# Where TensorE's side visits stand in a step, and a small matrix inverse in array tiles of 32 by 32

## The chip, the core and the metric

The kernel runs on one core of one Trainium2 chip. The metric is the device time of one execution in microseconds, as the median of several runs. A profiled execution shows each engine's instructions: TensorE (PE, and PEld for its weight loads), VectorE (DVE), ScalarE (ACT), GpSimd (POOL) and SyncE (SP), which issues most of the transfers.

## What is computed

Landmark (Nystrom) attention for 8 batches of 8 heads, then a dense two-layer network, then a mixture of 8 experts where each token goes to one expert.

```python
# attention, per batch and head: S = 576, D = 64, m = 32 landmarks
q_lm, k_lm = means of q and k over segments of 18
A, Bm, C = softmax(q k_lm^T), softmax(q_lm k_lm^T), softmax(q_lm k^T)
Z = Bm^T / (norm1(Bm) * norminf(Bm) + 1e-6)
for _ in range(6):
    Z = 2 * Z - Z @ Bm @ Z
x = A @ Z @ C @ v
# dense: (4608, 512) x (512, 2048), leaky relu 0.01, x (2048, 512)
# experts: argmax of x @ w_gate; out = gate * (relu(xe @ w1[e]) @ w2[e]), F = 1024
```

## The kernel before

TensorE's main work is a row of *steps*. A dense step ("m", 16 for each of 8 batches) does one 128-wide slice of the hidden layer: the first layer of the step two ahead (`h_mm`, L545, two halves of 288 columns, each of six matmuls) and then the second layer of this step (`o_mm`, L595, four *blocks* of 128 tokens, each of three matmuls: high by high, low by high, high by low). In batch 0 the second layer is plain fp32 (L590, one matmul per block). After each odd batch four short steps ("x", L604) finish the 64 tokens left over from two batches; then come the expert steps ("e", 8 per slot, with L899 for the first layer and L595, L921 for the second).

Everything else that TensorE does is a *visit*. The attention of batch b is cut into parts, and `PLAN` gives each a position in steps, counted from the start of batch b-1; `gate_plan` does the same for the gate's parts, and the tables at L1110 to L1122 for the experts' gathers. `side` turns the fraction of a position into a turn: an "m" step has 8, after each half of a half of the first layer (turns 0 to 3) and after each block (turns 4 to 7). An "e" step has 9, an "x" step 4. The engines execute in the order in which this loop writes, so a part that waits holds up whatever is written behind it on its engine.

The parts that matter here, for a batch b:

- `qk_load`, `red`: loads of q and k, and VectorE's sums over segments (L272), into `kT` and `qlm`
- `sc` 1 and `sc` 0: scores of landmarks against the keys' second and first half (L279, by `eight`), which need all of the reductions; `b_*` and `c_*`: softmax of them
- `et`, `tv`: transposes of C's scores (L365, L368) and C v (L378, 4 column tiles of 32)
- `n_g`, `n_k` 0 to 5, `n_y`, `n_w`: the inverse. Four heads lie on the partitions in groups of 32. To multiply four 32 by 32 matrices in one 128 by 128 matmul, VectorE spreads them into a block-diagonal matrix `rbd` with a mask `m4b` (L410, L437, L451, L458)
- `sa`, `a_*`: A's scores and softmax, transposed and split into `at`
- `u_mm`: the combined matrix times `w_in`, into `ub`, which the first layer of batch b reads; each takes two `wi` tiles, and loads the next two (`wi_load`)
- `xt_tr`, `logits`, `logits_t`, `g_l2`, `g_l3`, `g_l4`, `g_sc`: the gate of the batch before. `s_xt`: transposes of gathered expert tokens (L867)

Visits share two PSUM banks, `psw0` and `psw1` (from the experts on, one); the first layer has two, `hps`, and the blocks four. Batch 0's attention runs ahead of the steps, in the order of `FIRST`. Between its parts, and in the steps of batch 0, *ticks* convert the 64-bit weights: ScalarE L191 and L195, VectorE L199 and L203, GpSimd L216.

Of the kernel before, what the change touches and what calls it, by code (L numbers as in the profile page):

```python
# [66 lines left out]
def kernel(  # L67
# [100 lines left out]
    XE = 0.2  # L168
    XS = .4
# [231 lines left out]
    def b_nrm(b):  # L401
        bl, nn = A.pop((b, "bl")), A.pop((b, "nn"))
        bb = A[b, "bb"] = small("bb", [128, 2, 2, LM])
        DVE.tensor_reduce(out=nn[:, 2:4], in_=bl, axis=AX.X, op=ALU.add)
        DVE.tensor_scalar(out=nn[:, 2:4], in0=nn[:, 2:4], scalar1=1e-9, scalar2=None, op0=ALU.add)
        DVE.reciprocal(out=nn[:, 2:4], in_=nn[:, 2:4])
        DVE.tensor_tensor(out=bb[:, 0], in0=bl, in1=bcm(nn[:, 2:4]), op=ALU.mult)
        DVE.transpose(out=bb[:, 1].rearrange("p g m -> p (g m)"), in_=bb[:, 0].rearrange("p g m -> p (g m)"))
        rb = A[b, "rb"] = small("rbd", [128, 2, 4, LM], 2)
        DVE.tensor_tensor(out=rb, in0=bc4(bb[:, 1]), in1=m4b, op=ALU.mult)  # L410

    def n_g(b):
# [18 lines left out]
        DVE.tensor_tensor(out=gs, in0=ps[:, :2 * LM].rearrange("p (g m) -> p g m", g=2),  # L431
                          in1=bcm(cc), op=ALU.mult)
# [65 lines left out]

    PLAN = [
# [5 lines left out]
        (4.6, c_exp, 0), (4.75, c_exp, 1), (4.9, b_nrm), (5.2, c_rec, 0), (5.25, et, 0, 0), (5.26, et, 0, 1),
        (5.76, tv, 0), (5.77, et, 1, 0), (5.8, v_load, 1), (6.0, c_rec, 1), (6.26, et, 1, 1), (6.27, n_g),
        (6.76, sa, 0), (7.38, sa, 1), (7.7, a_max, 0), (7.75, a_sub, 0), (8.01, tv, 1), (8.02, n_k, 0),
        (8.25, a_exp, 0), (8.3, a_max, 1), (8.4, a_sub, 1), (8.63, n_k, 1), (8.8, a_sum, 0), (8.9, a_exp, 1),
        (9.0, a_mul, 0), (9.26, n_k, 2), (9.4, a_sum, 1), (9.5, a_mul, 1), (9.88, n_k, 3), (10.05, a_tr, 0),
        (10.2, a_hi, 0), (10.3, a_lo, 0), (10.51, n_k, 4), (10.7, a_tr, 1), (10.85, a_hi, 1), (10.95, a_lo, 1),  # L510
        (11.13, n_k, 5), (11.15, wi_load, 0), (11.3, wi_load, 1), (11.63, n_y), (12.13, n_w), (12.63, u_mm, 0),
        (13.88, u_mm, 2), (15.13, u_mm, 4), (18.13, u_mm, 6),
# [597 lines left out]
    for s in range(NSLOT):  # L1110
        t0 = T1 + NF * s
        x = t0 - 1 - XE - 5 * XS
        if s == 0:
            p = t_early + 0.4
        else:
            p = max(t_rest + 0.5 if s == KA else 0, x - 2.5)
        if s == 1:
            p = max(p, T1 - 2)
            x = max(x, p + 1)
        put([(p, part(s_tab, s))])  # L1120
        put([(p + 0.6 if j < XGB else x + XS * (j - XGB) + 0.1, part(s_gather, s, j)) for j in range(5)])
        put([(x + XS * j, part(s_xt, s, j)) for j in range(5)])  # L1122
# [169 lines left out]
```

## Time and profile before

| | us |
|---|---|
| median of 3 runs (1291.85 to 1292.27) | 1292.18 |
| the profiled execution | 1291.29 |
| its span | 1289.5 |
| TensorE busy in the span | 1227.5 (95%) |
| VectorE busy | 609.0 (47%) |
| ScalarE busy | 512.9 (40%) |
| GpSimd busy | 468.8 (36%) |

The span is what the profile's rows cover; 1.8 us of the execution lie around it. Matmuls overlap, each starting before the one before has left the array, so a step is best read from one start to the next. Of TensorE's busy time 383.8 us are L595 with `gh` and 253.4 us are L545. Times in the rows count from the start of the span.

### The profile page before, as it was taken

The page shows a single profiled execution, that of the slowest core. Times are in us where ns is not written, and L with a number is a line of the kernel's source. Part 1 is how long each engine was busy: PE and PEld are TensorE (multiplying, and loading weights), DVE is VectorE, ACT ScalarE, POOL GpSimd, SP SyncE. Part 2 cuts the span into 40 slices and gives each one's busy share as a digit, 9 for nine tenths or more (in the row PEclk, how much of TensorE's full clock was granted, in tenths as well). Part 3 has the DMA queues.
Part 4 walks back from the last instruction along what each step waited for, and adds up shares of the span by engine and source line. Part 5 has one row for each costly group of instructions (what it writes and reads, how often), then busy time and mean ns, then how long its engine had stood idle before and what let it go on. Part 6 is the DMA issues. An engine that isn't in the chain of part 4 may idle for free.

```text
span 1289.5 us, 22321 instructions
## 1 busy us (share of the span) xinstructions
PE 1227.5 (95%) x8630; PEld 1006.5 (78%) x8630; DVE 609.0 (47%) x1546; ACT 512.9 (40%) x1117; POOL 468.8 (36%) x362
## 2 busy tenths in 40 slices
PE   5788999999999999999999999999999999999994
PEld 2545567877877887878887888789989999999993
DVE  7788566535455435465435443244353332333311
ACT  3455355444344343344343444542343343333211
POOL 1544324433423424423424334624353333333201
PEclk9989999999999999999999999999999999999997
DMA  7677462351151241151141122341454334433001
GB/s 254 232 246 238 147 233 60 115 166 53 34 190 52 66 166 52 36 188 52 67 165 52 41 92 90 120 139 34 156 175 157 122 103 140 131 120 109 21 31 39
DMA packets 61891, 151.04 MB, mean 117 GB/s; under 512 B 10192, under 2 KB 19664, under 8 KB 61776
## 3 DMA queue, kind: packets, MB, share of 16 engines
q1 hardware_dynamic: 54736, 130.61, 30.8%
q0 software_dynamic: 7040, 18.92, 4.5%
q8 instruction: 70, 1.15, 0.4%
q14 instruction: 45, 0.37, 0.1%
HBM read 121.87 MB, written 27.63 MB: 116 GB/s over the span
## 4 chain that ended last, share of the span: by engine, by line
PE 79%; DVE 9%; issue 4%; ACT 1%; DMA 0%; POOL 0%; POOLq 0%; SPq 0%; DVEq 0%; ACTq 0%
PE acc L595 34%; PE hps L899 14%; PE hps L545 14%; PE psw L279 3%; PE acc L604 3%; PE psw L921 2%; PE acc L590 2%; PE psw L445 1%; PE psw L867 1%; PE psw L634 1%; DVE kT L272 1%; DVE qlm L272 1%; PE psw L378 1%; DVE te L199 1%; PE psw L642 1%
## 5 line engine op out<-in xcount | busy, mean ns | idle before, releaser
L595 PE MATMUL acc<-wo,gh 128*128 128x512 f32 x1216 | 383.8, 397 | 0.0
L562 POOL TENSOR_TENSOR gl<-hs,gh 128x512 fp32r<-128x512 f32 x112 | 147.1, 1313 | 311.5 <-ACT gh L561 183.2
L595 PEld LDWEIGHTS acc<-wo,gh 128*128 128x128 f32 x1216 | 217.6, 188 | 48.2 <-issue 11.7
L545 PE MATMUL hps<-at,ub 128*128 128x288 f32 x1536 | 253.4, 307 | 1.6 <-DVE hs L551 1.5
L545 PEld LDWEIGHTS hps<-at,ub 128*128 128x128 f32 x1536 | 220.9, 191 | 33.7 <-issue 20.0
L595 PE MATMUL acc<-wo,gl 128*128 128x512 f32 x608 | 238.0, 391 | 0.0
L551 DVE TENSOR_TENSOR hs<-hps,hs 128x288 f32<-128x288 f32 x224 | 98.9, 451 | 130.0 <-ACT hs L549 129.8
L908 DVE SCALAR_TENSOR_TENSOR gl<-hps,gh 128x288 fp32r<-128x288 f32 (+1 forms) x128 | 54.0, 423 | 197.3 <-ACT gh L904 197.3
L595 PEld LDWEIGHTS acc<-wo,gl 128*128 128x128 f32 x608 | 114.2, 188 | 25.0
L549 ACT ACTIVATE hs<-hps 128x288 f32<-128x288 f32 x256 | 101.9, 414 | 74.3 <-PE hps L545 71.1
L904 ACT ACTIVATE gh<-hps 128x288 fp32r<-128x288 f32 x128 | 52.8, 412 | 176.1 <-PE hps L899 111.6
L561 ACT CAST gh<-hs 128x512 fp32r<-128x512 f32 x112 | 69.5, 620 | 119.0 <-PE acc L595 94.4
L855 POOL DMA_INDIRECT xg<-x_d,gi x40 | 41.6, 1041 | 132.4 <-DVE gi L847 61.1
L940 POOL DMA_INDIRECT out_dram<-rows,gi x40 | 40.6, 1015 | 124.8 <-DVE rows L938 75.8
L492 DVE TENSOR_TENSOR ub<-psw,ub 128x512 fp32r<-128x512 f32 (+1 forms) x70 | 41.3, 632 | 70.0 <-ACT ub L491 70.0
L899 PE MATMUL hps<-xt,wo 128*128 128x288 f32 x480 | 68.7, 297 | 0.0
L899 PE MATMUL hps<-at,wo 128*128 128x288 f32 x480 | 68.0, 296 | 0.0
L899 PEld LDWEIGHTS hps<-xt,wo 128*128 128x128 f32 x480 | 66.4, 188 | 1.6
L899 PEld LDWEIGHTS hps<-at,wo 128*128 128x128 f32 x480 | 65.8, 188 | 1.6
L491 ACT CAST ub<-psw 128x512 fp32r<-128x512 f32 (+1 forms) x70 | 34.6, 547 | 65.6 <-PE psw L279 65.6
L595 PE MATMUL acc<-ub,gh 128*128 128x512 f32 x192 | 59.8, 393 | 0.0
L887 POOL TENSOR_TENSOR wo<-wraw,wo 128x1024 fp32r<-128x1024 f32 x20 | 48.0, 2398 | 23.3 <-ACT wo L883 23.0
(244 smaller groups left out, 1805.0 us busy)
## 6 DMA issues: line engine op xcount, KB each, us to landing
wraw<-in_moe_w_dram SPq DMA_DIRECT2D x64, 512.0 KB, 4.1
wi<-wi_d SPq DMA_DIRECT2D x56, 512.0 KB, 4.5
kT<-in_k_dram SPq DMA_DIRECT2D x32, 288.0 KB, 5.1
qT<-in_q_dram SPq DMA_DIRECT2D x32, 288.0 KB, 5.3
raw<-in_moe_w_in_dram SPq DMA_DIRECT2D x16, 512.0 KB, 5.2
vraw<-in_v_dram SPq DMA_DIRECT2D x16, 512.0 KB, 5.4
raw<-in_moe_w_out_dram SPq DMA_DIRECT2D x16, 512.0 KB, 4.6
x_d<-rows SPq DMA_DIRECT2D x32, 256.0 KB, 3.3
```

The source lines that it names most:

```text
L492: DVE.tensor_sub(out=u[:, :, 1, :], in0=p3, in1=u[:, :, 0, :].bitcast(F32))
L545: PE.matmul(out=ps[:, :HT], lhsT=us[:, wl, c:c + 128], rhs=at[:, al, 2 * (b % 2) + g, c0:c1], start=(n == 0), stop=(n == 5))
L549: ACT.mul(out=hs[:, c0:c1], in_=ps[:, :HT], mul=0.01)
L551: DVE.tensor_max(out=dst[:, c0:m], in0=ps[:, :m - c0], in1=hs[:, c0:m])
L561: ACT.copy(out=gh[:, :512], in_=src)
L562: POOL.tensor_tensor(out=gl, in0=src, in1=gh[:, :512].bitcast(F32), op=ALU.subtract)
L595: PE.matmul(out=acc(key, j), lhsT=g[hl][:, j * 128:(j + 1) * 128], rhs=wsel[:, wl, :], start=(f == 0 and i == 0), stop=(f == nf - 1 and i ...
L855: POOL.indirect_dma_start(out=xg[:n, :], out_offset=None, in_=x2_d[0:rows, :], in_offset=IND(ap=M[s, "gi"][:n, 0, j:j + 1], axis=0), bound ...
L887: (POOL if n % 2 else DVE).tensor_tensor(out=r[:, :, 1], in0=raw.rearrange("p (f c) -> p f c", f=2), in1=r[:, :, 0].bitcast(F32), op=ALU.s ...
L899: PE.matmul(out=ps[:, :HT], lhsT=wr[:, wl, d * 128:(d + 1) * 128], rhs=xt[:, al, d, c0:c1], start=(n == 0), stop=(n == 11))
L904: ACT.activation(out=gh[:, c0:c1], in_=ps[:, :HT], func=AF.Relu)
L908: DVE.scalar_tensor_tensor(out=lo, in0=ps[:, a - c0:b - c0], scalar=0.0, in1=gh[:, a:b].bitcast(F32), op0=ALU.max, op1=ALU.subtract)
```

## The change

Two things change. First, positions: in `PLAN`, `gate_plan` and the experts' table, visits of TensorE get positions that end in .51 or .88 (turn 4, behind the first block, and turn 7, behind the last), where they had any turn. Their other parts move along. Second, the inverse is no longer done with block-diagonal matrices. `diag` multiplies the four heads' 32 by 32 matrices as four matmuls, each on its own rows and columns of the array (partitions 32p to 32p+32), which write one PSUM bank at different partitions. The addition of the former Z is a further matmul with the identity `C["eye"]`, accumulated in PSUM, and one ScalarE copy takes the result out; VectorE's masked copies, copies and additions in `n_k` are gone, and the masks in `b_nrm` and `n_g`. `FIRST` is the same.

```diff
+    def diag(out, lhs, rhs, start=True, stop=True):
+
+        for p in range(4):
+            h = slice(32 * p, 32 * p + 32)
+            PE.matmul(out=out[h], lhsT=lhs[h], rhs=rhs[h], start=start, stop=stop, skip_group_check=True)
...
     def n_k(b, i):
-        rx, rb = A[b, "rx"], A[b, "rb"]
+
+        rx = A[b, "rx"]
         lo, hi = {0: (0, 1), 5: (1, 2)}.get(i, (0, 2))
         ps = psw()
         for g in range(2):
-            PE.matmul(out=ps[:, 64 * g + LM * lo:64 * g + LM * hi], lhsT=rb[:, g].rearrange("p h m -> p (h m)"),
-                      rhs=rx[:, g, lo:hi, :])
-        p4 = ps[:, :128].rearrange("p (g a m) -> p g a m", g=2, a=2)
-        nx = small("rx", [128, 2, 2, LM], 2)
-        nb = small("rbd", [128, 2, 4, LM], 2)
-        if i < 5:
-            DVE.tensor_tensor(out=nb, in0=bc4(p4[:, :, 0, :]), in1=m4b, op=ALU.mult)
-            DVE.tensor_copy(out=nx[:, :, 0, :], in_=p4[:, :, 0, :])
-        if i > 0:
-            DVE.tensor_tensor(out=nx[:, :, 1, :], in0=p4[:, :, 1, :], in1=rx[:, :, 1, :], op=ALU.add)
-        else:
-            DVE.tensor_copy(out=nx[:, :, 1, :], in_=rx[:, :, 1, :])
-        if i == 5:
-            DVE.tensor_tensor(out=nb, in0=bc4(nx[:, :, 1, :]), in1=m4b, op=ALU.mult)
-        A[b, "rx"], A[b, "rb"] = nx, nb
+            c, m, e = 64 * g + LM * lo, 64 * g + LM, 64 * g + 2 * LM
+            diag(ps[:, c:c + LM * (hi - lo)], rx[:, g, 0, :], rx[:, g, lo:hi, :], stop=hi == 1)
+            diag(ps[:, m:e], C["eye"], rx[:, g, 1, :], start=hi == 1)
+        nx = A[b, "rx"] = small("rx", [128, 2, 2, LM], 2)
+        ACT.copy(out=nx[:, :, lo:, :], in_=ps[:, :128].rearrange("p (g a m) -> p g a m", g=2, a=2)[:, :, lo:, :])
...
-        (3.625, sc, 1), (4.125, sc, 0), (4.0, b_max), (4.3, c_max, 0), (4.5, c_max, 1), (4.52, b_exp),
+        (3.88, sc, 1), (4.2, b_max), (4.4, b_exp), (4.88, sc, 0), (5.05, c_max, 0), (5.15, c_exp, 0), (5.2, c_max, 1),
...
-        P += [(t, g_l2), (t + 0.1, g_l3), (2.88 + NX * (b % 2), g_l4), (3.4 + NX * (b % 2), g_sc)]
+        P += [(t, g_l2), (t + 0.1, g_l3), (3.51 + NX * (b % 2), g_l4), (4.0 + NX * (b % 2), g_sc)]
...
-        x = t0 - 1 - XE - 5 * XS
+        xp = [t0 + x for x in (-3.45, -3.08, -2.45, -2.08, -1.45)]
```

Three places show how the order moves, all in batch 5, which carries batch 6's attention.

TensorE at `sc` half 1, before. `acc0` to `acc3` are the step's blocks, `hps` its first layer, `psw` the visit's banks; the visit's eight matmuls (two banks, four heads' `kT`) stand as their first and last:

```order
L545 MATMUL hps_6344<-at_84,ub_83 128x288 x6
L595 MATMUL acc0_6144<-wo1_1560,gh_6252 128x512 x2
L595 MATMUL acc0_6144<-wo1_1560,gl_6253 128x512
L595 MATMUL acc1_6150<-wo1_1560,gh_6252 128x512 x2
L595 MATMUL acc1_6150<-wo1_1560,gl_6253 128x512
L279 MATMUL psw0_6372<-kT_6109,qlm_6218 32x320
...
L279 MATMUL psw1_6373<-kT_6172,qlm_6218 32x320
L595 MATMUL acc2_6156<-wo1_1560,gh_6252 128x512 x2
```

The same place of TensorE after, with `g_l4`'s two matmuls (L679, L680) in the same step:

```order
L580 MATMUL acc0_6581<-wo1_1710,gl_6688 128x512
L679 LDWEIGHTS ltri_b_87
L679 MATMUL psw1_6792<-oh_6705,ltri_b_87 128x32
L680 LDWEIGHTS ones_b_88
L680 MATMUL psw1_6792<-ohc_6706,ones_b_88 128x32
...
L580 MATMUL acc3_6612<-wo1_1710,gl_6688 128x512
L276 MATMUL psw0_6816<-kT_6559,qlm_6661 32x320
...
L276 MATMUL psw1_6817<-kT_6610,qlm_6661 32x320
L530 MATMUL hps_6839<-at_84,ub_83 128x288 x6
```

The visit moved from behind the second block to behind the fourth, and `g_l4` into its step, behind the first block.

VectorE ahead of that visit, before: the last two reductions (L272) stand behind `g_l4`'s eight instructions (L702 to L710), the first and last of which are shown:

```order
L272 TENSOR_REDUCE qlm_6218<-qT_6154 128x32
L702 TENSOR_REDUCE pay_6319<-gex_6237 128x4
...
L706 TENSOR_TENSOR grk_6316<-psw1_6313,cst_81 128x32
...
L710 CAST gpi_6318<-gpf_6317 128x4
L272 TENSOR_REDUCE kT_6172<-kT_6172 128x32
L551 TENSOR_TENSOR hs_6333<-hps_6334,hs_6333 128x288
L272 TENSOR_REDUCE qlm_6218<-qT_6178 128x32
```

VectorE at the same place after:

```order
L269 TENSOR_REDUCE kT_6610<-kT_6610 128x32
L536 TENSOR_TENSOR hs_6768<-hps_6769,hs_6768 128x288
L269 TENSOR_REDUCE qlm_6661<-qT_6628 128x32
L536 TENSOR_TENSOR hs_6768<-hps_6779,hs_6768 128x288
L687 TENSOR_REDUCE pay_6798<-gex_6704 128x4
...
L691 TENSOR_TENSOR grk_6795<-psw1_6792,cst_81 128x32
```

The reductions moved ahead of the gate's chain.

TensorE between the first and the second `u_mm` of that batch, before (from the last matmul of the one to the first of the other):

```order
L279 MATMUL psw0_6952<-wi_6892,wt_86 32x256
L595 MATMUL acc2_6156<-wo6_2325,gh_6864 128x512 x2
L595 MATMUL acc2_6156<-wo6_2325,gl_6865 128x512
L595 MATMUL acc3_6174<-wo6_2325,gh_6864 128x512 x2
L595 MATMUL acc3_6174<-wo6_2325,gl_6865 128x512
L545 MATMUL hps_6989<-at_84,ub_83 128x288 x6
L545 MATMUL hps_6998<-at_84,ub_83 128x288 x6
L595 MATMUL acc0_6144<-wo6_2325,gh_6917 128x512 x2
...
L595 MATMUL acc3_6174<-wo6_2325,gl_6918 128x512
L279 MATMUL psw1_7019<-wi_6973,wt_86 32x256
```

The same stretch of TensorE after:

```order
L276 MATMUL psw0_7483<-wi_7390,wt_86 32x256
L530 MATMUL hps_7514<-at_84,ub_83 128x288 x6
L530 MATMUL hps_7523<-at_84,ub_83 128x288 x6
L580 MATMUL acc0_6581<-wo6_2434,gh_7442 128x512 x2
...
L580 MATMUL acc3_6612<-wo6_2434,gl_7443 128x512
L276 MATMUL psw1_7544<-wi_7504,wt_86 32x256
```

Six blocks between the two visits became four. In the same way the inverse's steps, one visit each, moved to turns 4 and 7; there two matmuls became sixteen, of 64 and of 32 columns. In the trace each fp32 matmul is two records.

## Rows read from the trace of the kernel before

**Rows 1.** Stretches: length, busy us (instructions) of each engine, clock, transfers.

```profile
14.00:46.50 32.50, 18.55 (x191) 13.16 (x191) 28.25 (x73) 13.96 (x30) 12.47 (x10) 1.00 0.58 196
46.50:141.00 94.50, 83.82 (x531) 49.55 (x524) 76.40 (x177) 50.07 (x110) 44.73 (x34) 0.95 0.71 235
141.00:820.00 679.00, 671.53 (x5189) 539.38 (x5190) 341.13 (x934) 290.64 (x710) 247.24 (x199) 1.00 0.30 101
```

**Rows 2.** TensorE in order of time (start, us, what), batch 6's `sc` visits.

```profile
577.93 0.76 PE L279 MATMUL psw<-kT,qlm 64*32 64x320 f32 x12
...
580.58 0.73 PE L595 MATMUL acc<-wo,gh 128*128 128x512 f32 x2
...
582.96 0.72 PE L279 MATMUL psw<-kT,qlm 64*32 64x288 f32 x16
583.60 0.66 PE L545 MATMUL hps<-at,ub 128*128 128x288 f32 x3
```

**Rows 3.** TensorE in order of time, the first and last of the six visits.

```profile
191.93 1.16 PE L279 MATMUL psw<-kT,qlm 64*32 64x320 f32 x12
...
195.33 0.73 PE L595 MATMUL acc<-wo,gh 128*128 128x512 f32 x2
...
680.58 0.76 PE L279 MATMUL psw<-kT,qlm 64*32 64x320 f32 x12
...
682.58 0.74 PE L595 MATMUL acc<-wo,gh 128*128 128x512 f32 x2
```

**Rows 4.** VectorE in order of time, ahead of that visit.

```profile
575.86 0.18 DVE L702 TENSOR_REDUCE pay<-gex 128x4 f32<-128x32 f32 x1
...
578.09 0.75 DVE L272 TENSOR_REDUCE kT<-kT 128x32 f32<-128x576 f32 x1
```

**Rows 5.** VectorE in order of time, one step of batch 0's inverse.

```profile
29.50 0.42 DVE L451 TENSOR_TENSOR rbd<-acc,cst 128x256 f32<-128x256 f32 x1
29.84 0.21 DVE L452 COPY rx<-acc 128x64 f32<-128x64 f32 x1
...
30.10 0.74 DVE L300 TENSOR_REDUCE amx<-st 128x18 f32<-128x576 f32 x1
```

**Rows 6.** A stretch behind a long wait of TensorE, as in rows 1.

```profile
91.00:97.00 6.00, 6.00 (x52) 3.00 (x51) 2.06 (x7) 2.55 (x6) 2.59 (x2) 0.67 0.13 49
```

**Rows 7.** TensorE in order of time, first and second `u_mm` of batch 6.

```profile
629.63 1.09 PE L279 MATMUL psw<-wi,wt 64*32 64x256 f32 x32
...
632.15 1.76 PE L545 MATMUL hps<-at,ub 128*128 128x288 f32 x12
633.75 0.62 PE L595 MATMUL acc<-wo,gh 128*128 128x512 f32 x2
...
636.26 0.39 PE L595 MATMUL acc<-wo,gl 128*128 128x512 f32 x1
636.58 1.09 PE L279 MATMUL psw<-wi,wt 64*32 64x256 f32 x32
637.61 1.86 PE L545 MATMUL hps<-at,ub 128*128 128x288 f32 x12
639.30 0.63 PE L595 MATMUL acc<-wo,gh 128*128 128x512 f32 x2
```

**Rows 8.** SP's issue of two `wi` tiles; landing of all from 200 to 800.

```profile
637.35 0.80 SPq L238 DMA_DIRECT2D wi<-wi_d  x2
...
DMA to landing us min/median/max: 3.5/4.5/5.9
```

**Rows 9.** TensorE in order of time, around one step of batch 6's inverse.

```profile
608.67 0.39 PE L595 MATMUL acc<-wo,gl 128*128 128x512 f32 x1
...
609.81 0.39 PE L595 MATMUL acc<-wo,gl 128*128 128x512 f32 x1
```

**Rows 10.** A stretch within one `tv` visit, as in rows 1.

```profile
591.52:591.97 0.45, 0.45 (x33) 0.44 (x32) 0.00 (x0) 0.00 (x0) 0.00 (x0) 1.00 0.00 0
```

**Rows 11.** TensorE in order of time, in batch 7's remainder steps.

```profile
831.13 0.66 PE L634 MATMUL psw<-cst,rows 128*128 128x128 f32 x4 [2.04 <-DVE xt L870]
```

More of the change, by code (lines that the diff above doesn't have):

```diff
@@ L160, in wo @@
         return wo_t[f // 2][:, f % 2]
-    XE = 0.2
-    XS = .4
     XGB = 3
@@ L408, in b_nrm @@
         DVE.transpose(out=bb[:, 1].rearrange("p g m -> p (g m)"), in_=bb[:, 0].rearrange("p g m -> p (g m)"))
-        rb = A[b, "rb"] = small("rbd", [128, 2, 4, LM], 2)
-        DVE.tensor_tensor(out=rb, in0=bc4(bb[:, 1]), in1=m4b, op=ALU.mult)
     def n_g(b):
-        bb, rb = A[b, "bb"], A.pop((b, "rb"))
-        ps = A[b, "gps"] = psw()
+        bb = A[b, "bb"]
+        ps = psw()
         for g in range(2):
-            PE.matmul(out=ps[:, g * LM:(g + 1) * LM], lhsT=rb[:, g].rearrange("p h m -> p (h m)"),
-                      rhs=bb[:, 1, g, :])
+            diag(ps[:, 64 * g:64 * g + LM], bb[:, 1, g, :], bb[:, 1, g, :])
         nn = small("nn2", [128, 2, 2])
         DVE.tensor_reduce(out=nn, in_=bb, axis=AX.X, op=ALU.add)
-        nbt = small("rbd", [128, 2, 4, LM], 2)
+        nbt = small("nbt", [128, 2, 4, LM])
         nb, nt = nbt[:, 0], nbt[:, 1]
@@ L430, in n_g @@
         gs = small("bl", [128, 2, LM])
-        DVE.tensor_tensor(out=gs, in0=ps[:, :2 * LM].rearrange("p (g m) -> p g m", g=2),
+        DVE.tensor_tensor(out=gs, in0=ps[:, :128].rearrange("p (g m) -> p g m", g=2)[:, :, :LM],
                           in1=bcm(cc), op=ALU.mult)
@@ L503 @@
         (2.4, red, 'k', 2), (2.65, red, 'q', 2), (3.0, red, 'k', 3), (3.25, red, 'q', 3),
-        (3.625, sc, 1), (4.125, sc, 0), (4.0, b_max), (4.3, c_max, 0), (4.5, c_max, 1), (4.52, b_exp),
[L505 to L512, printed above, removed]
+        (3.88, sc, 1), (4.2, b_max), (4.4, b_exp), (4.88, sc, 0), (5.05, c_max, 0), (5.15, c_exp, 0), (5.2, c_max, 1),
+        (5.3, b_nrm), (5.4, c_exp, 1), (5.6, c_rec, 0), (5.88, et, 0, 0), (5.89, et, 0, 1),
+        (6.51, tv, 0), (6.52, et, 1, 0), (6.55, v_load, 1), (6.7, c_rec, 1), (6.88, et, 1, 1), (6.89, n_g),
+        (7.51, sa, 0), (8.51, sa, 1), (8.7, a_max, 0), (8.75, a_sub, 0), (8.88, tv, 1), (8.89, n_k, 0),
+        (9.1, a_exp, 0), (9.15, a_max, 1), (9.25, a_sub, 1), (9.51, n_k, 1), (9.6, a_sum, 0), (9.7, a_exp, 1),
+        (9.8, a_mul, 0), (9.88, n_k, 2), (10.1, a_sum, 1), (10.2, a_mul, 1), (10.51, n_k, 3), (10.6, a_tr, 0),
+        (10.88, n_k, 4), (10.9, a_hi, 0), (11.0, a_lo, 0), (11.15, wi_load, 0), (11.2, a_tr, 1), (11.3, wi_load, 1),
+        (11.51, n_k, 5), (11.6, a_hi, 1), (11.7, a_lo, 1), (11.88, n_y), (12.51, n_w), (12.88, u_mm, 0),
+        (13.88, u_mm, 2), (14.88, u_mm, 4), (18.51, u_mm, 6),
     ]
@@ L1115 @@
         else:
-            p = max(t_rest + 0.5 if s == KA else 0, x - 2.5)
+            p = max(t_rest + 0.5 if s == KA else 0, xp[0] - 2.5)
         if s == 1:
             p = max(p, T1 - 2)
-            x = max(x, p + 1)
+            xp = [max(x, p + 1 + i / 100) for i, x in enumerate(xp)]
         put([(p, part(s_tab, s))])
-        put([(p + 0.6 if j < XGB else x + XS * (j - XGB) + 0.1, part(s_gather, s, j)) for j in range(5)])
-        put([(x + XS * j, part(s_xt, s, j)) for j in range(5)])
+        put([(p + 0.6 if j < XGB else xp[j - XGB] + 0.1, part(s_gather, s, j)) for j in range(5)])
+        put([(xp[j], part(s_xt, s, j)) for j in range(5)])
     def first_u0(_, s):
```

25 lines of the change are left out of this document (9 added, 16 removed).

## Prediction

> **What bounds the kernel now.** I read the table of stretches first. From 141 to 820 us TensorE is busy 671.53 of 679.00 us, so there only what TensorE executes and waits for counts. Before that it is not the bound: VectorE is busy 28.25 of 32.50 us from 14 to 46.5 us (87%, TensorE 57%), and 76.40 of 94.50 us from there to 141 us (81%) [rows 1]. The first stretch is the inverse of batch 0 with the conversion of the weights; the second is plain batch 0, with batch 1's attention and the rest of the conversion beside it. So the change is costed by two rules: VectorE's instructions before 141 us, TensorE's spacing after it.
>
> In the TensorE-bound part I read visits from start to start, because matmuls overlap and "idle" shows only part of a stall. One visit per batch waits for long: `sc` with half 1. In the fifth of the six steady batches (2 to 7) it holds the blocks back from 577.93 to 580.58 us, 2.65 us, where the other half, which waits for nothing, takes 582.96 to 583.60, 0.64 us [rows 2]. The first takes 3.40 us and the last 2.00 us [rows 3]; the four between are 2.00, 2.64, 2.00 and 2.65. VectorE's last `qlm` ends the wait, and it is late because the gate's `g_l4` chain, from 575.86 to 578.09 us, 2.23 us, stands in VectorE's queue ahead of the last two reductions [rows 4]. Together the six waits cost 14.69 - 6 x 0.64 = 10.85 us; half 1 is 32 columns wider, which takes off some 0.3: **10.5 us**.
>
> **The change part by part.**
>
> *Removed VectorE work.* A full step of the iteration occupies VectorE from 29.50 to 30.10 us, 0.60 us: the masked copy 0.34, the copy and the addition 0.13 each [rows 5]. Per attention the change takes away four such steps (2.40), step 0 (mask, two copies: 0.60), step 5 (addition and mask: 0.47) and two more masks (0.68), 4.15 us in all; ScalarE gets six small copies, and has room. For batch 0 all this lies in the stretch where VectorE is busy 87% of the time, so I take 0.87 x 4.15 = 3.6 us: **-3.6** (bounds 0, if the chain through ScalarE and TensorE takes over, and -4.2). For batch 1, 0.81 x 4.15 = 3.4 us, less some of TensorE's added work (below): **-3.0**. Its bounds are wide, since all visits of batch 1 also move, most of them later: +2 if VectorE then waits for TensorE's results, -7 if the long stalls go too; after one of them TensorE runs 6 us at a granted 0.67 of its clock, between its levels of 1.2 and 2.4 GHz, where 1.00 would need 4 us [rows 6]. From batch 2 on VectorE's saving is worth nothing, as TensorE sets the pace.
>
> *`sc` moved.* Half 1 goes from behind a step's second block to behind its fourth, 2 x 0.68 = 1.37 us later, and `g_l4` goes behind the last reduction, which takes 2.23 us out of its way. Together 3.6 us, more than the longest wait of 2.76. What is late next is the PSUM bank: `g_l4` now holds one of the two `psw` banks three blocks before `sc` wants both, and VectorE reads it some 1.8 us into its chain. I leave 0.3 us for that: **-10.2** (bounds -10.5 and -6, if the bank costs most of a microsecond each time).
>
> *`u_mm` moved.* The second and third of these visits come one step after the one before. Now 629.63 to 636.58, 6.95 us, holds a step and two blocks more. A step without a visit takes 636.58 - 632.15 = 4.43 us, the visit itself 637.61 - 636.58 = 1.03 [rows 7], so the new spacing is 5.5 us. Their `wi` tiles are asked for 0.77 us after the visit starts (637.35 against 636.58), the second 0.45 later, and land 4.5 us after issue, 5.9 at most [rows 8]: the second is there 5.7 to 7.1 us after the visit's start, and is wanted at 5.5 + 0.5 = 6.0. SP's queue is not otherwise held. That is 0 to 1.1 us of waiting, twice in each of six batches; the median says nothing, the maximum 1.1, and I take 0.3: **+3.5** (0 to +13).
>
> *The inverse in array tiles.* A step's visit now costs TensorE 609.81 - 608.67 = 1.14, less three matmuls at 0.228: 0.46 us [rows 9]. It was 4 matmul records; steps 0 to 5 become 32 records, `n_g` and `n_y` 16, each on one of four diagonal tiles. No row shows 32 by 32 tiles. The nearest is `tv`, four column tiles side by side: 32 weight loads and matmuls of 64 columns in 0.45 us, so a round of four takes 56 ns [rows 10]. The fixed price of a visit in tiles I take from `u_mm`: 636.26 to 639.30 is 3.04, less a plain first layer (633.75 - 632.15 = 1.60) and one matmul (0.23): 1.21 us; its four rounds of 256 columns take 0.89 at `tv`'s rate, which leaves 0.32 [rows 7]. So steps 1 to 4 cost 0.32 + 4 x 0.056 + 4 rounds of 32 columns at 0.028 to 0.056, 0.66 to 0.77: +0.20 to +0.31 each. Step 5 is +0.08 to +0.31, `n_y` about 0, step 0 (behind `tv`) and `n_g` (behind `et`) -0.05 to +0.25 each. Sum per batch +0.75 to +2.1; I take 1.2, nearer the low end because `tv`'s rounds go with its columns. Times six: **+7.2** (+4.5 to +12.6).
>
> *Expert steps.* `s_xt` moves from between first-layer quarters to behind blocks. Only stalls can change: one of 2.04 us in batch 7's remainder steps [rows 11], where three transposing visits still share two banks. **-0.5** (-2.3 to +1.5).
>
> Sum: -3.6 - 3.0 - 10.2 + 3.5 + 7.2 - 0.5 = -6.6 us. The profiled execution took 1291.29 us, 0.89 below the median of 1292.18, so **1285.6 us** as a median. Its own range, the bounds taken together but not all at one end: 1279 to 1289.5.
>
> **The rivals.**
>
> *Array tiles that don't run side by side (slower).* The four diagonal tiles take different rows of the array and write one PSUM bank. `eight`, the only helper that uses two row groups, gives each its own bank, so no row shows four row groups on one. If they went in turn, a round would cost four times as much: steps 1 to 4 1.66 to 2.11 us, +1.2 to +1.65 each; steps 0 and 5 +0.75 to +1.65; `n_g` and `n_y` +0.3 to +0.75. That is 6.9 to 11.4 us a batch, 41 to 68 in place of 7.2: **1319 to 1346**. It decides from 0.3 us more per step on. Against it: `tv`'s four tiles share a bank and run together, as they write different partitions, which the diagonal tiles do too. The Trainium skill, "TensorEngine Tiling (Array Packing)", Restrictions and Gotchas, says that different row tiles write to different PSUM banks and cannot access the same one at once. By that rule this rival is what happens; no trace here bears on it. Chance 0.10.
>
> *`wi` late at its upper end, and the tiles at theirs (slower).* A landing of 5.9 us each time gives +13, and tiles at 56 ns for every round +12.6: 1285.6 + 9.5 + 5.4 = **1300**; half of it is 1293 and more. For it: the landing was measured with the transfers spread wider. Against: the median of 4.5. Chance 0.10.
>
> *Nothing gained before 141 us (no change).* TensorE and ScalarE chains take over where VectorE is relieved; the two early terms are 0: 1285.6 + 6.6 = **1292.2**. For it: VectorE already idles 18.1 us of the second stretch. Against: in the first it idles 4.3 of 32.5 us. Chance 0.14.
>
> *All goes well (faster).* `wi` never late, tiles at their low end, the early stretch 2 us better: 1285.6 - 3.5 - 2.7 - 2 = **1277**. Chance 0.12.
>
> **How the numbers follow.** The forecast has 0.54. A measurement of this kernel can tell about 0.2%, 2.6 us, from no change. Faster by more than that: 0.54 + 0.12 = 0.66. Within it: 0.14. Slower: 0.10 + 0.10 = 0.20. The range goes from 1275, a little below the best case, to 1298, which takes in most of the late `wi` case and leaves out the tiles in turn (0.10) and some 0.07 at both ends.
>
> **What would show it.** `sc` half 1 should take 0.7 us from start to start in all steady batches; if over 1.5 remain, the term of 10.2 is wrong. The visit of step 1 to 4 should cost 0.66 to 0.77 us; 1.6 is the first rival. `u_mm`'s second and third visit should show waits for the `wi` transfer of a few tenths. The first matmul of plain batch 0 (46.5 us now) should come 3 to 4 us earlier, and the point at which VectorE ceases to be the bound (141 us) some 6 us earlier. The prediction fails if the early gain is not there or if visits in tiles cost over 0.9 us.

## The result, and the profile after

The changed kernel takes 1277.45 us (median of 4 runs, 1275.73 to 1278.30) against 1292.22 for the kernel before: a ratio of 0.9879, with a 95% interval of 0.9861 to 0.9897. That is 15 us less. The forecast was 1285.6, 6.6 us less, so the direction held and the time lies inside the range, but the gain is more than twice the one that was worked out.

Both kernels run the same 5632 matmuls of the two layers in the same order. So the traces can be laid beside each other by the start of the same matmul, and the difference splits by stage. The first column (prologue) is the time up to the first matmul of plain batch 0, the second goes from there to the 361st (which starts at 174.07 us before and 159.80 after), the third (steady batches) to the 3121st (815.36 and 804.10), the last (experts) to the start of the last one:

| us against the kernel before | prologue | stage of plain batch 0 | steady batches | experts | sum |
|---|---|---|---|---|---|
| forecast | -3.6 | -3.0 | +0.5 | -0.5 | -6.6 |
| the changed kernel | -4.8 | -9.5 | +3.0 | -3.2 | -14.4 |

The rows that answer to [rows 1], the same stretches of the changed kernel (length, busy us and instructions of TensorE, its weight loads, VectorE, ScalarE and GpSimd, granted clock, transfers):

```profile
14.00:46.50 32.50, 18.86 (x405) 13.53 (x406) 28.06 (x62) 17.16 (x41) 16.40 (x12) 0.63 0.62 199
46.50:141.00 94.50, 89.48 (x788) 50.58 (x787) 77.33 (x164) 51.94 (x117) 42.26 (x32) 0.98 0.75 250
141.00:820.00 679.00, 672.51 (x6307) 524.88 (x6305) 316.28 (x809) 299.89 (x751) 249.49 (x201) 1.00 0.31 101
```

These stretches are cut at the same times, so the changed kernel, which is ahead, has more of its work in the second one, and busy times there can't be compared. Cut at the same matmuls (the 1st to the 253rd, rows in the first experiment below) VectorE is busy 77.0 us before and 75.3 after and idle 18.5 and 10.1, and TensorE idle 10.8 and 5.3. Most of the gain there is not VectorE's work, it is less waiting on both. The third stretch is full in both.

What became of the steady batches is read visit by visit, as the time from start to start less the same matmuls without a visit. `sc`'s half 1, 2.65 us in [rows 2], now goes through at once (changed kernel, TensorE in order of time: start, length, what):

```profile
566.94 0.77 PE L276 MATMUL psw<-kT,qlm 64*32 64x320 f32 x16
567.64 1.59 PE L530 MATMUL hps<-at,ub 128*128 128x288 f32 x10
...
603.71 0.40 PE L580 MATMUL acc<-wo,gl 128*128 128x512 f32 x1
604.04 0.31 PE L387 MATMUL psw<-rx 32*32 32x64 f32 x8
604.18 0.24 PE L387 MATMUL psw<-rx,cst 32*32 32x32 f32 x8
604.24 0.29 PE L387 MATMUL psw<-rx 32*32 32x64 f32 x8
604.35 0.24 PE L387 MATMUL psw<-rx,cst 32*32 32x32 f32 x8
604.52 0.74 PE L580 MATMUL acc<-wo,gh 128*128 128x512 f32 x2
605.10 0.40 PE L580 MATMUL acc<-wo,gl 128*128 128x512 f32 x1
...
605.80 0.39 PE L580 MATMUL acc<-wo,gl 128*128 128x512 f32 x1
```

The visit is 567.64 - 566.94 = 0.70 us, as in five of the six steady batches. In the first it takes 1.45 us (from 178.65); there `g_l4`'s chain on VectorE starts only 0.04 us ahead of it, so the bank that the prediction named may be held, which is not shown. The rows below it are around one step of the inverse in tiles: 16 records of 64 columns and 16 of 32 in turn, within the 0.48 us from 604.04 to 604.52. From the `gl` at 603.71 to the one at 605.10 it is 1.39 us, where the next one follows 0.70 later, so the visit costs 0.69 us (0.46 in [rows 9]).

By kind of visit, in the steady batches: `sc` 21.00 to 11.09 us (-9.9), the steps of the inverse 13.60 to 19.98 (+6.4, and -0.3 for step 0 behind `tv`), `u_mm` 30.59 to 33.25 (+2.7), the other visits +0.1 together, and +4.0 that are in no visit at all, most of them in first layers. What TensorE waited for between 160 and 804 us (changed kernel: us in total, times, longest):

```profile
PE hps L530 <- DVE csm L352: 2.4, 4, 0.7
PE psw L276 <- DMA wi<-wi_d: 1.8, 3, 0.8
PE hps L530 <- DVE hs L536: 1.5, 1, 1.5
```

The first row is new (the third stands in the kernel before as well, 1.5). Its cause is in the rows of all engines in order of time (changed kernel, TensorE's, VectorE's and GpSimd's around one of the four):

```profile
291.67 0.46 DVE L536 TENSOR_TENSOR hs<-hps,hs 128x288 f32<-128x288 f32 x1 [0.59 <-issue]
...
291.88 0.97 POOL L705 DMA_INDIRECT tab_d<-pay,gpi  x1 [0.30 <-issue]
292.04 0.21 DVE L404 TENSOR_REDUCE nn<-bl 128x2 f32<-128x64 f32 x1
...
292.29 1.92 DVE L405 TENSOR_SCALAR nn<-nn 128x2 f32<-128x2 f32 x1
...
292.86 1.30 POOL L547 TENSOR_TENSOR gl<-hs,gh 128x512 fp32r<-128x512 f32 x1
...
293.60 1.04 PE L530 MATMUL hps<-at,ub 128*128 128x288 f32 x6
...
294.87 0.42 DVE L536 TENSOR_TENSOR hs<-hps,hs 128x288 f32<-128x288 f32 x1
295.21 0.13 DVE L352 TENSOR_SCALAR csm<-csm 128x1 f32<-128x1 f32 x1
295.34 0.40 PE L530 MATMUL hps<-at,ub 128*128 128x288 f32 x1 [0.70 <-DVE csm L352]
```

VectorE reads the second half of a first layer (L536) only at 294.87, since `b_nrm` (L404 to L408) stands ahead of it, and one instruction of `b_nrm` on two columns lasts 1.92 us. It ends at 294.21, when GpSimd's subtraction ends (292.86 + 1.30 = 294.16). TensorE, whose next half needs that bank, stands still for 0.70 us. (The view names L352, the instruction that ends as TensorE starts; the bank's reader is L536, just ahead of it.)

### The profile page after: what moved, and what is told of

The parts are those of the page before. It is cut to its first block, busy times and chain, and to the rows that moved or that the text cites. A ratio compares the mean times of both kernels' runs of the same rounds, so it can differ in the third digit from the quotient of the medians.

```text
span 1275.0 us, 25218 instructions
## 1 busy us (share of the span) xinstructions
PE 1223.1 (96%) x10166; PEld 982.3 (77%) x10166; DVE 581.0 (46%) x1394; ACT 520.6 (41%) x1165; POOL 470.3 (37%) x362
## 4 chain that ended last, share of the span: by engine, by line
PE 83%; issue 5%; DVE 4%; DMA 1%; ACT 1%; POOL 0%; ACTq 0%; POOLq 0%; DVEq 0%
PE acc L580 35%; PE hps L530 15%; PE hps L884 14%; PE psw L276 4%; PE acc L589 3%; PE acc L575 3%; PE psw L906 2%; PE psw L387 2%; PE psw L852 1%; DMA wi<-wi_d 1%; PE psw L619 1%; PE psw L375 1%; PE psw L627 1%; DVE nn L405 1%; DVE csm L343 1%
## 5 line engine op out<-in xcount | busy, mean ns | idle before, releaser
L530 PE MATMUL hps<-at,ub 128*128 128x288 f32 x1536 | 238.5, 304 | 5.2 <-DVE csm L352 3.0
L530 PEld LDWEIGHTS hps<-at,ub 128*128 128x128 f32 x1536 | 212.3, 189 | 31.7 <-issue 19.1
L536 DVE TENSOR_TENSOR hs<-hps,hs 128x288 f32<-128x288 f32 x224 | 98.3, 454 | 153.6 <-ACT hs L534 150.0
L872 POOL TENSOR_TENSOR wo<-wraw,wo 128x1024 fp32r<-128x1024 f32 x20 | 51.1, 2554 | 31.2 <-ACT wo L868 30.9
```

The costliest lines, as they stand in the source:

```text
L530: PE.matmul(out=ps[:, :HT], lhsT=us[:, wl, c:c + 128], rhs=at[:, al, 2 * (b % 2) + g, c0:c1], start=(n == 0), stop=(n == 5))
L536: DVE.tensor_max(out=dst[:, c0:m], in0=ps[:, :m - c0], in1=hs[:, c0:m])
L872: (POOL if n % 2 else DVE).tensor_tensor(out=r[:, :, 1], in0=raw.rearrange("p (f c) -> p f c", f=2), in1=r[:, :, 0].bitcast(F32), op=ALU.s ...
```

## Experiments

Each kernel was timed beside the kernel before, and laid beside it by the same matmuls. All of them:

| us against the kernel before, in the trace | prologue | stage of plain batch 0 | steady | experts | sum | ratio of times, interval |
|---|---|---|---|---|---|---|
| the changed kernel | -4.8 | -9.5 | +3.0 | -3.2 | -14.4 | 0.9879 (0.9861 to 0.9897) |
| e1_moves | -0.3 | -4.5 | -0.9 | -2.5 | -8.2 | 0.9949 (0.9933 to 0.9966) |
| e2_tiles | -4.3 | -0.8 | +7.8 | +0.3 | +3.0 | 1.0000 (0.9991 to 1.0010) |
| e3_old_batch1 | -4.8 | -2.6 | +2.3 | -3.1 | -8.2 | 0.9951 (0.9935 to 0.9966) |
| e9_et_old | -4.7 | -8.7 | +3.2 | -3.2 | -13.3 | 0.9891 (0.9874 to 0.9908) |
| e11_rest_old | -4.5 | -5.6 | +2.3 | -3.2 | -11.0 | 0.9912 (0.9895 to 0.9928) |
| e8_gate_early | -4.8 | -9.0 | +1.7 | -1.9 | -14.1 | 0.9885 (0.9869 to 0.9902) |
| e10_old_experts | -4.8 | -8.7 | +3.3 | -0.7 | -10.9 | 0.9909 (0.9892 to 0.9926) |
| e4_umm_apart | -4.3 | -9.1 | -1.0 | -3.2 | -17.6 | 0.9867 (0.9851 to 0.9884) |
| e5_nrm | -4.9 | -11.1 | 0.0 | -3.2 | -19.1 | 0.9867 (0.9851 to 0.9883) |
| e6_masks_late | -4.7 | -8.2 | -2.0 | -3.2 | -18.0 | 0.9859 (0.9842 to 0.9875) |
| e12_umm_nrm | -4.5 | -8.1 | -2.5 | -3.2 | -18.2 | 0.9860 (0.9838 to 0.9881) |
| e7_all | -4.8 | -8.0 | -8.8 | -2.4 | -24.1 | 0.9807 (0.9790 to 0.9823) |

The stages come from one execution each. In the stage of plain batch 0 such executions differ by up to 1.5 us where nothing was edited: in e6, which is the changed kernel up to batch 1, one first layer and the two blocks behind it, from 97 us, take 1.4 us longer, at a granted clock of 0.50 against 0.80 from 96.9 to 102 us (e7 and e12 show the same). So differences below 1.5 us are not read there. e2's traced execution is the slowest of its ten, 3.4 us above their median, so its stages add up to +3.0 where its times say 0; e5's is the fastest of its four, 2.5 us below.

### Moves and tiles apart

```
e1_moves: before's inverse (masks, four matmuls a step), with the changed
          PLAN, gate_plan and positions of s_xt
e2_tiles: the changed inverse (diag, ScalarE's copy), with before's
          PLAN, gate_plan and positions of s_xt
```

> All moves of the change (positions of the visits, gate and transposing visits), with the kernel before's inverse: block-diagonal left sides, masks on VectorE, four matmuls a step. Theory M (batch 1's stage gains because its visits stand later and farther apart, so that TensorE's long waits for VectorE go): the prologue gains 0, the stretch from the first plain-batch matmul to main matmul 360 gains about 9, the steady batches 3.1 (the 3.0 that the changed kernel lost there plus the 6.1 of its tiles back), the expert part 3.2: -15, about 1277 us. Theory V (it gains because VectorE's masks and copies are gone): that stretch gains only some 1.5, -7.8 in all, about 1284.5.

> The inverse in tiles of 32 by 32 alone, every visit where the kernel before has it. Both theories: the prologue gains 4.8 us, the steady batches lose 6.1. Theory M: the stretch of plain batch 0 gains only some 0.5, so +0.8, about 1293 us, with TensorE's waits behind et and sa still there. Theory V: it gains some 8, so -6.7, about 1285.5.

Measured: 1283.24 us (the kernel before 1290.16 beside it) and 1290.80. Neither theory holds. The moves alone give 4.5 us in the stage of plain batch 0, where theory M wanted 9 and theory V 1.5; the tiles alone give 0.8, where theory V wanted 8 (if all the 3.4 us by which that execution was slow lay in this stage, it would be 4.2); together they give 9.5. The prologue belongs to the tiles (-4.3 of -4.8) and the expert part to the moves (-2.5 of -3.2). In the steady batches the moves gain less than their expected 3.1, as first layers wait 4.9 us longer than before and `u_mm` costs 3.2 more, and the tiles cost more than 6.1, as `sc`'s wait grows by 1.0. Alone, the tiles are worth nothing: what they gain in the prologue they lose in the steady batches.

The stage can be read in three pieces, cut at the same matmuls (the 1st, 109th, 169th and 253rd): `et`, `n_g` and a `u_mm` lie in the second, most of the inverse in the third. The kernel before, with the columns of [rows 1]:

```profile
46.49:78.73 32.24, 30.81 (x163) 18.88 (x157) 25.62 (x56) 17.37 (x39) 15.36 (x12) 1.00 0.87 301
78.73:109.12 30.39, 24.40 (x180) 13.76 (x179) 22.50 (x58) 16.47 (x39) 10.12 (x9) 0.88 0.73 233
109.12:141.96 32.84, 29.45 (x198) 17.73 (x197) 28.87 (x65) 16.50 (x34) 20.23 (x16) 0.95 0.52 165
```

e1, the moves alone:

```profile
46.22:77.11 30.89, 29.41 (x163) 17.77 (x157) 25.86 (x57) 17.59 (x38) 14.67 (x12) 1.00 0.88 303
77.11:101.99 24.88, 21.06 (x164) 12.02 (x163) 23.36 (x55) 16.09 (x38) 10.21 (x8) 1.00 0.86 279
101.99:136.48 34.49, 30.30 (x210) 17.50 (x209) 29.65 (x67) 15.72 (x34) 20.09 (x15) 0.96 0.54 183
```

e2, the tiles alone:

```profile
42.16:74.45 32.29, 30.79 (x163) 18.93 (x157) 25.61 (x56) 17.48 (x39) 15.34 (x12) 0.93 0.86 300
74.45:104.19 29.74, 24.45 (x192) 13.42 (x191) 21.47 (x56) 16.25 (x38) 9.93 (x9) 0.89 0.71 238
104.19:136.86 32.67, 29.40 (x367) 17.17 (x365) 28.68 (x49) 17.32 (x41) 20.42 (x16) 0.95 0.51 167
```

The changed kernel:

```profile
41.72:72.76 31.04, 29.30 (x163) 18.05 (x157) 25.83 (x57) 17.50 (x38) 14.67 (x12) 0.96 0.89 305
72.76:98.09 25.33, 21.88 (x176) 12.32 (x175) 23.34 (x55) 16.58 (x39) 11.16 (x9) 0.95 0.87 283
98.09:127.05 28.96, 28.84 (x350) 16.50 (x349) 26.10 (x47) 15.54 (x35) 16.20 (x13) 0.99 0.55 184
```

VectorE's idle time over the three pieces (length less its third busy number) is 18.5 us before, 18.9 in e2, 11.4 in e1 and 10.1 after; its busy time is 77.0, 75.8, 78.9 and 75.3. So neither engine was full. What VectorE waited for over the three pieces (two rows each of the kernel before and of the changed one):

```profile
DVE te L199 <- ACT te L191: 5.2, 4, 1.8
DVE tn L383 <- PE psw L378: 3.4, 2, 2.7
...
DVE tn L380 <- PE psw L375: 0.8, 1, 0.8
DVE te L196 <- ACT te L188: 0.6, 1, 0.6
```

The waits form a ring of three engines. In the kernel before, TensorE's transposes `et` wait 3.48 us for VectorE's `ub` (until 89.68), ScalarE's copy of them 2.25 us for TensorE (until 90.83), and VectorE 1.22 us for a `te` that ScalarE writes behind that copy (until 92.72). The moves end most of it: the two waits are 0.6 (`te`) and 1.2 (`tn`) in e1, 4.5 and 4.0 in e2. A part of the gain may come with the clock, which was lower behind a long wait ([rows 6]): length times what the granted clock lacks of 1.00 adds up, by the rows above, to 5.3 us before, 7.2 in e2, 1.4 in e1 and 2.8 after. As an estimate, that is the most that the clock can have cost.

The gain in the middle piece is the moves' (30.39 to 24.88 us in e1). The last one needs both: 34.49 us with the moves alone, 32.67 with the tiles alone, 28.96 with both. The waits of TensorE say why. The kernel before, from 97 to 142 us (one of 3.5 us ahead of `et` comes before):

```profile
PE psw L279 <- DVE st L290: 2.5, 1, 2.5
PE psw L445 <- DVE ub L492: 2.5, 2, 2.1
PE psw L279 <- DVE rx L454: 0.6, 1, 0.6
```

e1 over the second and third piece:

```profile
PE psw L445 <- DVE rx L454: 3.3, 3, 2.2
PE psw L279 <- DVE bl L431: 2.0, 1, 2.0
PE hps L545 <- DVE csm L355: 1.1, 1, 1.1
```

e2 over the same:

```profile
PE psw L389 <- DVE ub L478: 3.3, 2, 1.7
PE psw L364 <- DVE ub L478: 3.0, 1, 3.0
PE psw L278 <- DVE st L289: 2.3, 1, 2.3
```

At the old positions (before and e2) a visit of batch 1 wants a `psw` bank that VectorE has yet to read: `ub` is read from a `u_mm`'s result, `st` from `sa`'s. The moves let VectorE read it in time. But then the inverse's step waits for its own chain on VectorE (`rx`, 3.3 us in e1), the masked copies, and it is the tiles that take those out. In the changed kernel no such wait is left in the third piece.

### Which positions of batch 1

```
e3_old_batch1, e9_et_old, e11_rest_old:
-                for pos, fn, *a in PLAN]
+                for pos, fn, *a in (PLAN1 if b == 1 else PLAN)]
PLAN1 is the changed PLAN with before's positions of
  e3: all visits        e9: sc up to et        e11: sa up to u_mm
```

> The changed kernel, but batch 1's attention (the one that stands beside plain batch 0) has its visits at the positions of the kernel before. Theory M: the stretch of plain batch 0 gives its gain back, +8 to +9 against the changed kernel, about 1286 us. Theory V: +1.5 at most, about 1279.

> The changed kernel, with batch 1's first group of visits alone (sc to et, with their reductions and b_nrm) at the positions of the kernel before: et at 5.25 in place of 5.88. Its other visits, and all other batches, stay as changed. With the whole of batch 1 at the old positions the stretch of plain batch 0 lost 6.9 us, 6.0 of it in the 12 main matmuls around et. If et comes too early for VectorE (its psw banks hold u_mm's result, whose reading stands behind two reductions and b_nrm): some 6 of it come back, about 1282 us (ratio to before 0.992 to 0.993), with a wait of some 3 us ahead of et, in one piece. If it is the sum of many small waits of the whole batch: 1 to 2 us, about 1278.5.

> The changed kernel, with batch 1's second group alone (sa, the second part of tv, the steps of the inverse, u_mm) at the positions of the kernel before; its first group up to et and n_g stays as changed. The whole batch at old positions cost 6.9 us in the stretch of plain batch 0; the first group alone 0.9, though et's wait of 3.0 us was back. If each collision on a psw bank has its own price: the rest, +6, about 1281.5 (ratio to before 0.992 to 0.993), with TensorE's waits ahead of u_mm (2.3) and in the inverse (3.3) back. If a wait only passes to the next visit unless all of them are moved: +1 to +3, about 1278 to 1279.

Measured: 1283.20 us for e3 (ratio 0.9951), 1277.66 for e9 (0.9891), 1280.33 for e11 (0.9912). With batch 1 back at the old positions 6.9 of the stage's 9.5 us are gone. The first group alone costs 0.8, less than executions differ by, the second 3.9: the rest of the 6.9 needs both. The case of e9 teaches most. TensorE's waits in it, from 76 to 100 us:

```profile
PE psw L362 <- DVE ub L476: 3.0, 1, 3.0
PE psw L276 <- DVE bl L428: 0.6, 1, 0.6
...
```

And the changed kernel in the same stretch:

```profile
PE psw L276 <- DVE bl L428: 2.0, 1, 2.0
PE hps L530 <- DVE csm L352: 0.6, 1, 0.6
...
```

The wait of 3.0 us ahead of `et` is back, as in the kernel before (3.5, the longest of all), and at the 145th matmul TensorE stands 4.2 us behind the changed kernel. Yet at the 169th it is only 1.2 behind: the wait ahead of the next `u_mm`, 2.0 us in the changed kernel, has shrunk to 0.6, and the first-layer wait is gone. While TensorE stood still, VectorE worked off its queue. So a wait of 3.0 us cost 0.8 us by the stages and nothing that the times can tell (1277.66 against 1277.45). In e11 the waits of the inverse's steps (L387) are back:

```profile
PE psw L387 <- DVE ub L476: 3.3, 2, 1.7
...
PE psw L387 <- DVE st L287: 0.6, 1, 0.6
```

Its other waits in the stage add up to 4.6 us, those of the changed kernel to 5.2. So here 3.9 us of waiting cost 3.9 us: these were worth about their length.

### What ended sc's wait

```
-(3.51 + NX * (b % 2), g_l4), (4.0 + NX * (b % 2), g_sc)
+(2.88 + NX * (b % 2), g_l4), (3.4 + NX * (b % 2), g_sc)
```

> The changed kernel with the gate's g_l4 and g_sc back at 2.88 and 3.4; sc stays behind the fourth block. It tells which of the two moves ended sc's wait of 9.9 us. If 1.37 us later is most of it: the waits of 2.76, 2.00, 1.36, 2.00, 1.36 and 1.36 us shrink by 1.37 each, so about +2.7 in all, 1280. If VectorE's queue is what counts, g_l4's 2.23 us come back at each: +6 to +9, 1283 to 1286. If sc's position is enough by itself: 0, 1277, or less, since GpSimd's scatters then stand earlier and the long b_nrm instruction goes.

Measured: 1277.30 us, ratio 0.9885: no change against the changed kernel. With the gate's `g_l4` early again `sc`'s visits cost 0.6 us more in all, of the 9.9 that were gained. So the place of `sc` is enough: the last `qlm` ends 0.17 us after the start of the visit of [rows 2] in e8 and 1.93 us after it in the kernel before, with `g_l4` ahead of it in both. In the same trace the long `b_nrm` instruction is 0.17 us in every steady batch and the first-layer waits are gone (-3.4), so it is `g_l4`'s and `g_sc`'s move that brought them; `g_l4`'s own visits (+0.6), `wi` (+0.8) and the expert part (+1.3) take that back.

### The expert part

```
-        xp = [t0 + x for x in (-3.45, -3.08, -2.45, -2.08, -1.45)]
+        x = t0 - 1 - XE - 5 * XS
```

> The changed kernel with the experts' transposing visits (s_xt and the loads tied to them) at the positions of the kernel before, between first-layer quarters. The expert part gained 3.2 us: 2.35 by the first expert's first layers and 1.7 at the third expert's, less 0.9 elsewhere. If these positions are all of it: the two waits come back and +3.2, about 1280.5 (ratio to before 0.990 to 0.991). If the first 2.35 come from the gate's visits of the last batch, which moved as well: +0.8 to 1.7 alone, about 1278.5 to 1279.

Measured: 1280.25 us, ratio 0.9909. The expert part keeps 0.7 of its 3.2 us, so these positions are most of it. Waits are back where the changed kernel has none over 0.6 (e10, TensorE from 805 us on):

```profile
PE psw L621 <- DVE xt L857: 2.0, 1, 2.0
PE psw L854 <- DVE xt L857: 1.8, 2, 1.0
```

The first is the stall of [rows 11]. Of the two in the second row, one has a like in the kernel before, 1.0 us at 945.81, in the third expert.

### What the changed kernel lost, and a version without it

```
e4_umm_apart: -(13.88, u_mm, 2), (14.88, u_mm, 4)
              +(14.51, u_mm, 2), (16.02, u_mm, 4)
e5_nrm:       -(5.3, b_nrm)
              +(6.1, b_nrm)
e6_masks_late: n_g, n_k, n_y and the last mask of b_nrm
              as in the kernel before if b >= 2, in tiles if b < 2
e7_all: e4, e5 and e6 together        e12_umm_nrm: e4 and e5
```

> The changed kernel with the second and third u_mm visit at 14.51 and 16.02 instead of 13.88 and 14.88, so that there are two blocks more for the wi transfers. If the lateness of wi is what the spacing costs (waits of 0.16 to 1.06 us seen at four of these visits), -2.7 us, about 1274.7, and no wait for wi left. If the waits only turn into waits for a psw bank or for the wi buffers: within 0.7 of 1277.4.

> The changed kernel with one visit moved: b_nrm, VectorE's normalisation of the landmark block, from 5.3 to 6.1 of a step's positions. In the changed kernel TensorE's first layers wait for an hps bank at 190.9, 294.3, 487.5 and 681.4 us, 0.39, 0.87, 0.86 and 0.87 us, with 0.11 behind each. Theory N: VectorE reads that bank late because b_nrm's five instructions stand ahead of it, one of them (two columns, 0.17 us elsewhere) lasting 1.59 to 1.93 us while GpSimd runs its subtraction. Then the four waits are gone and the instruction lasts 0.17 to 0.7: -3.4 us, about 1274 (ratio to before some 0.985). Rival: the wait goes to the next reading of an hps bank, or n_g finds its operand late: 0 to +2, 1277 to 1279.

> The changed kernel, with its tiles of 32 by 32 for batches 0 and 1 alone; from batch 2 on the inverse is the kernel before's (masks on VectorE, four matmuls a step), at the changed kernel's positions. If tiles pay where VectorE is the bound and cost where TensorE is: prologue and stage of plain batch 0 as in the changed kernel (-4.8 and -9.5 against before), the steady batches as with the moves alone (-0.9 in place of +3.0): -3.9 against the changed kernel, about 1273.5. By the price of the visits alone (0.685 against 0.46 us) it would be -6.1, about 1271. Rival: VectorE's masks bring its queue back to where TensorE waits for it: 0 or worse, 1277 and up.

> Three edits of the changed kernel together: u_mm's visits at 14.51 and 16.02, b_nrm at 6.1, and tiles in the inverse for batches 0 and 1 alone. If the three act on separate waits: -3.2 - 3.4 - 3.9 = -10.5 against the changed kernel, about 1267 (ratio to before 0.980). If VectorE's queue is the common cause behind them, the gains overlap: -5 to -7, 1270 to 1272.

> Two of the three edits of e7_all: u_mm's visits at 14.51 and 16.02 and b_nrm at 6.1, with the tiles kept in all batches. If the masks from batch 2 on are worth their -6.5 + 0.6 + 0.3 us of visits there once the first-layer waits are gone, this is 5 to 6 us slower than e7_all: about 1272.5, ratio to before 0.984 to 0.985. If masks and spacing overlap: 1269 to 1270.

Measured: 1273.83, 1274.38, 1273.61, 1267.34 and 1273.40 us. In e4 `u_mm`'s visits are back at 30.71 us (33.25 after, 30.59 before) and no wait for `wi` is left, so its lateness was the price of the closer spacing; 1.5 us of the first-layer waits went too. In e5 the two-column instruction lasts 0.17 us from batch 2 on, and of the four first-layer waits two are left, at 0.4: -3.0 us in the steady batches by the trace, -1.6 by the ratio of times, whose interval of 0.0016 to either side can't tell the two. In e6 the steady batches gain 5.0 us over the changed kernel: 6.5 from the steps and 1.7 at `u_mm` (why there is not shown), less 0.9 for `n_y` and step 0 and 2.3 for longer first-layer waits, as VectorE has the masks to do again.

The three together take 1267.34 us, 0.9807 (0.9790 to 0.9823) of the kernel before and faster than the changed kernel, whose interval ends at 0.9861. The expectation was 1267. e12, the same with tiles in all batches, is 6.3 us longer in the steady batches (-2.5 against -8.8): tiles pay in batches 0 and 1, where masks stand in VectorE's way, and cost from batch 2 on. TensorE's waits of e7 from 161 to 800 us are a single one, which the kernel before has too:

```profile
PE hps L606 <- DVE hs L612: 1.6, 1, 1.6
```

## Why the prediction was right in direction and wrong in size

The terms against what the trace shows:

| us | forecast (bounds) | measured |
|---|---|---|
| masks of batch 0 | -3.6 (0 to -4.2) | -4.8 |
| masks of batch 1, its visits moved | -3.0 (+2 to -7) | -9.5 |
| `sc` | -10.2 (-10.5 to -6) | -9.9 |
| `u_mm` and `wi` | +3.5 (0 to +13) | +2.7 |
| the inverse in tiles | +7.2 (+4.5 to +12.6) | +6.1 |
| in no visit, most of it first layers waiting for VectorE | not there | +4.0 |
| expert steps | -0.5 (-2.3 to +1.5) | -3.2 |

**The step that failed** is "For batch 1, 0.81 x 4.15 = 3.4 us, less some of TensorE's added work (below): -3.0". It took VectorE's busy share in the stretch for the part of its work that sets the time. But with the masks gone and nothing moved (e2) the stage gains 0.8 us, and with the moves and the masks kept (e1) 4.5. An engine that is busy 81% and stands still in waits of up to 2.7 us isn't the bound; its work counts only where another engine waits for it. The prediction had named the long stalls as a bound ("-7 if the long stalls go too") and [rows 6] as their trace, and set them aside. They did go, and the bound was too near, as it counted no more than the stalls at TensorE and their clock, while the stage holds VectorE's idle time too, 18.5 us of which 8.4 went. The moves alone free 7.1 of them (e1), and only on top of the moves do the tiles take 3.6 us off VectorE's busy time there (78.9 to 75.3).

**First layers.** The prediction listed `g_l4`'s move for what it frees and not for what it puts behind it: on GpSimd's queue its scatters now stand ahead of a subtraction, which then meets `b_nrm` on VectorE, ahead of a reading of `hps`. That cost 3.4 of the 4.0 us: so much is gone in e8, where `g_l4` and `g_sc` are back. Where the rest lies is not shown.

**Expert steps.** The size was off: the one stall of 2.04 us was counted at a quarter, and a second of 1.0 us was not in the rows. Both went.

**Right.** The prologue, a little past its bound (e2 gives 4.3 with the tiles alone): from 14 us to the first matmul of plain batch 0 VectorE's busy time went from 28.24 to 24.57 us, 3.7 less where 3.6 was said, and its idle time fell by 1.1 as well. `sc` to 0.3 us, though e8 shows that the half of its reason with `g_l4` wasn't needed, `wi` late by a few tenths at some visits, and the tiles' visit, 0.69 us where 0.66 to 0.77 was said. Its parts hold too: two rounds of 64 columns take 0.11 us (604.24 to 604.35) and two of 32 columns 0.06 (604.18 to 604.24), so eight rounds 0.34, which leaves 0.35 for the way in and out where 0.32 was said.

**The rivals.** Tiles in turn: a round of the four diagonal tiles with 64 columns takes 55 ns, as long as a round of `tv`'s four column tiles (56 ns, [rows 10]), so they run side by side on one bank, and the step costs 0.69 us and not 1.66 to 2.11. The Trainium skill, "TensorEngine Tiling (Array Packing)", Restrictions and Gotchas, says that different row tiles cannot access the same PSUM bank at once. These rows differ from it, and show no cost of it. Late `wi` at its upper end: 2.7 of 13. Nothing before 141 us: refuted by both early columns. "All goes well" has the time that came, 1277, but not for its reasons: `wi` was late (+2.7) and the tiles cost more than their low end (6.1 against 4.5); the early stretch was 8 us better rather than 2.

## What to carry to other kernels

Where two in-order engines feed each other, a busy share of 80% does not make either the bound: look for the waits that alternate, and change positions and work together, since here each alone gave 0.8 and 4.5 us and both 9.5. The longest wait is not the dearest one: 3.0 us ahead of `et` cost 0.8 us or less, as the engine that was waited for used the time and the next wait shrank. Of a visit that is moved, follow every queue that it touches to the instruction that now stands behind it, and use a form that relieves one engine at the cost of another only in the stage where that engine is the one waited for (tiles in two batches of eight, e7).

## What the runs showed of the hardware

A VectorE instruction on 128x2 elements that takes 0.17 us elsewhere lasts 1.59 to 1.93 us in four places of the changed kernel, and ends within 0.05 us of a GpSimd subtraction of two SBUF operands (292.29 + 1.92 against 292.86 + 1.30, that is 294.21 and 294.16; at another of the four 188.71 + 1.59 against 188.96 + 1.30, 190.30 and 190.26). The Trainium skill, "SBUF — State Buffer", "SBUF: two separate sides", says that a pair of ports is an exclusive lock between GpSimd and those VectorE instructions that run in a two-port mode or have two SBUF inputs: whichever starts first gets it for its whole instruction, and the other blocks. The ends agree with that; whether this instruction runs in such a mode is not shown. The order does not, by the recorded starts: VectorE's row starts 0.57 and 0.25 us ahead of the subtraction's, while GpSimd's scatter (291.88 + 0.97) is still running. A scatter alone needn't hold it, as in e1 the same instruction took 0.17 us within one (300.89, in 300.63 to 301.60). What holds it until the subtraction starts is not shown.

TensorE's mean granted clock from 14 to 46.5 us is 0.63 in the changed kernel, between its levels of 1.2 and 2.4 GHz, and 1.00 before ([rows 1]). From 14 to 42 us it is 0.61, and 0.83 in e2, whose prologue has the same tiles (384 records of TensorE against 383, busy 14.4 us against 14.7); why these two differ is not shown. The prologue is 4.3 to 4.8 us shorter all the same, as VectorE sets its pace (in the changed kernel it is busy 24.57 of the 27.72 us from 14 us to the first matmul of plain batch 0, TensorE 14.38).

Tiles of 32 by 32 in four row groups write one PSUM bank side by side, and their price goes with the columns: a round of four takes 55 ns with 64 columns and 30 ns with 32 (604.18 to 604.35, two rounds of each).
